# Earlier FFN jobs, a two-engine final projection and a re-searched prologue in a fused attention and FFN kernel

## The chip, the cores and the metric

The kernel runs on one core of a Trainium2 chip. Times are device microseconds (us) of one execution. A kernel's time is the median of its runs. The span of a profile runs from the first to the last instruction and is 1.7 to 1.9 us shorter than the time of the same run. Engines are written as in the profile: PE is TensorE's matmul pipe, PEld its weight loads, DVE is VectorE, ACT is ScalarE, POOL is GpSimd, SP issues DMAs (SPq is its queue).

## The reference

```python
x = A_x                                    # [1, 2048, 640] bf16
xn = layernorm(x)                          # over the last axis
# A: 32 query heads of 20, one shared key and value head (multi-query attention)
q = (xn @ wq) split in 32 heads;  k = xn @ wk;  v = xn @ wv
o = softmax(q k^T / sqrt(20)) v            # 32 x 2048 x 2048 scores
# B: FFN of width 1728
h = silu(xn @ w1)
return x + o @ wo + h @ w2
```

## The kernel before

The kernel is a generator. A scheduler in Python holds a cost model for each engine, decides for every engine a fixed order of instructions, and emits these orders with semaphores. On the chip nothing is decided any more: where the head of DVE's order, a reciprocal, waited 4.35 us in the changed kernel and began at 62.64, the phase copy behind it began only at 62.78.

The work is cut into 688 score steps (the queries of up to three heads against one block of 128 keys). For each, PE makes scores (L749 in the profile), ACT takes the exponential (L767), DVE takes over one head in many steps by an integer trick (L781, with phase copies in L842), and PE sums exponentials times values (L830). Sixteen key blocks make one group. Its sums U are evacuated by DVE, transposed by a DMA and normalised on POOL and DVE. In what follows this transpose is called the sum transpose. It is one DMA on SP's queue:

```python
    def norm_dma(self, g, rows):
        ...
        op = sc.dma("sp", lambda q: q.dma_start_transpose(self.UT[:, up, :, 0:rows], self.U[0:rows, up, :]),
                    [("U", up)], [("UT", up)], rows * QW * 2, sem=self.s_UT[up], name="uTd")
        ...      # four POOL instructions form sums and denominators in W, then on DVE:
        sc.new("dve", 0.22, lambda v: v.reciprocal(rl, w[:, :, :, DH]), [("W", 0), ("W", 1)], [("rL", up)],
               prio=U_PRIO, name=f"rcp{g}")
```

The prologue loads x, takes the statistics of 16 tiles of 128 rows, gets reciprocal square roots by Newton steps in batches of four tiles, normalises, transposes each tile (on PE, or by a DMA for the tiles in `DT`), and makes keys, values and queries. Then SP issues the loads of w1, wo, x (for the residual) and, last, the 14 pieces of w2 (2.2 MB). Fourteen DVE fills write a constant into the query buffer. Filler matmuls (L673, L686) stand where PE has no other work.

The end of the kernel, before: the FFN part and four fifths of the last chunk's projection are added by DVE into `yx`. After the last normalising, the last slice of `o` is transposed on PE and copied by DVE; then eight last-slice matmuls follow, and DVE adds all eight to `yx`:

```python
        if c == QC - 1:
            for i in range(4):
                for e in range(2):
                    self.misc.append(self.out_job(c, i, e, ffn=False, ks=range(DC - 1), src="yx", dst="yx"))
            self.misc.append(self.oT_last_job(c))
            for i in range(4):
                for e in range(2):
                    self.misc.append(self.out_job(c, i, e, ffn=False, ks=range(DC - 1, DC), src="yx"))
```

The softmax here doesn't subtract the row's maximum and nothing guards it: scores larger than these inputs give would overflow.

## Time and profile before

| | first set | with the changed kernel |
|---|---|---|
| median | 744.6 us (3 runs) | 744.75 us (4 runs) |
| range | 743.72 to 744.91 | 743.72 to 745.08 |
| profiled run | 747.35 us, span 745.6 | |

### The profile page before, as it was taken

To read this page: it belongs to the slowest core of one execution; us is meant where nothing else is said; L and a number is where in the kernel's file an instruction comes from. 1 tells how busy PE (TensorE), PEld (TensorE's weight loads), DVE (VectorE), ACT (ScalarE), POOL (GpSimd) and SP (SyncE) were. 2 spreads that over 40 slices of the span, in tenths; PEclk is the share of its full clock that TensorE was granted. 3 is DMA by queue.
4 is the path that set the end of the run, shared out by engine and by line. 5 is a ranking of instruction groups with operands and counts; after the bars stand their busy time and mean duration, and the time that the engine had idled before them with its cause. 6 is when DMAs were issued, how large, how long until landed. Compare 5 with 4: busy or idle time off the path is not lost.

```text
span 745.6 us, 17784 instructions
## 1 busy us (share of the span) xinstructions
PE 721.1 (97%) x6781; PEld 230.5 (31%) x6781; DVE 713.9 (96%) x1397; ACT 707.9 (95%) x780; POOL 111.7 (15%) x280
## 2 busy tenths in 40 slices
PE   8889999999999999999999999999999999999996
PEld 4332222233332222223333232222333322233332
DVE  7978999999999999999999999999999999999997
ACT  8968999999999999999999999999999999999962
POOL 5421112011112111110120111111111121111100
PEclk9979999999999999999999999999999999999999
DMA  6660000101003110000011211000002110000021
GB/s 188 158 248 15 17 20 16 22 16 15 9 15 62 52 46 16 9 16 1 8 16 25 70 44 37 16 8 8 10 8 43 51 45 8 8 9 8 9 43 36
DMA packets 55961, 27.05 MB, mean 36 GB/s; under 512 B 43686, under 2 KB 55238, under 8 KB 55878
## 3 DMA queue, kind: packets, MB, share of 16 engines
q1 hardware_dynamic: 54566, 25.87, 13.7%
q8 instruction: 55, 0.90, 0.5%
q10 hardware_dynamic: 1312, 0.05, 0.1%
q14 instruction: 28, 0.23, 0.1%
HBM read 11.36 MB, written 2.62 MB: 19 GB/s over the span
## 4 chain that ended last, share of the span: by engine, by line
PE 51%; DVE 20%; ACT 19%; issue 5%; POOL 2%; DMA 2%; DVEq 0%; ACTq 0%; POOLq 0%; SPq 0%
ACT sbt L767 18%; PE psall L830 17%; PE psall L749 17%; DVE sbt L781 9%; PE psall L1057 6%; PE psall L1119 5%; DVE sbt L842 5%; PE psall L1023 2%; PE psall L1124 2%; PE psall L673 2%; DVE sbt L1070 1%; DMA sbt<-sbt 1%; ACT sbt L1065 1%; DVE sbt L945 1%; DVE sbt L1352 1%
## 5 line engine op out<-in xcount | busy, mean ns | idle before, releaser
L767 ACT ACTIVATE sbt<-psall 128x1024 bf16<-128x1024 f32 (+2 forms) x688 | 674.4, 1117 | 21.7 <-PE psall L749 18.1
L781 DVE TENSOR_SCALAR sbt<-psall 128x512 int16<-128x512 f32 x608 | 406.4, 684 | 16.5 <-PE psall L749 10.2
L749 PE MATMUL psall<-sbt 32*128 32x512 bf16 x2048 | 269.5, 385 | 12.0 <-ACT sbt L767 6.0
L830 PE MATMUL psall<-sbt 128*32 128x512 bf16 x3434 | 264.7, 387 | 0.0
L842 DVE TENSOR_SCALAR sbt<-sbt 128x1536 int16<-128x1536 int16 (+2 forms) x436 | 223.9, 533 | 1.5
L749 PEld LDWEIGHTS psall<-sbt 32*128 32x128 bf16 x2048 | 69.7, 91 | 252.8 <-issue 86.8
L830 PEld LDWEIGHTS psall<-sbt 128*32 128x32 bf16 x3434 | 67.2, 95 | 112.4 <-issue 75.1
L915 POOL CAST sbt<-sbt 128x168 f32<-128x168 bf16 x42 | 17.3, 411 | 522.0 <-DMA sbt<-sbt 522.0
L1119 PE MATMUL psall<-sbt 128*128 128x320 bf16 x448 | 86.8, 303 | 0.0
L1057 PE MATMUL psall<-sbt 128*128 128x512 bf16 (+1 forms) x280 | 83.6, 384 | 1.6 <-DVE sbt L1070 1.0
L1119 PEld LDWEIGHTS psall<-sbt 128*128 128x128 bf16 x448 | 34.0, 97 | 43.4 <-issue 34.8
L1070 DVE SCALAR_TENSOR_TENSOR sbt<-sbt,psall 128x512 bf16<-128x512 bf16 (+1 forms) x56 | 38.2, 682 | 1.6 <-ACT sbt L1065 0.8
L931 POOL TENSOR_TENSOR sbt<-sbt 128x240 bf16<-128x240 f32 (+2 forms) x44 | 27.9, 635 | 65.7 <-DVE sbt L922 51.1
L1065 ACT ACTIVATE sbt<-psall 128x512 bf16<-128x512 f32 (+1 forms) x56 | 37.6, 671 | 0.0
L1124 PE MATMUL psall<-sbt 128*128 128x320 bf16 x160 | 31.6, 303 | 1.0 <-DVE sbt L1102 0.7
L1057 PEld LDWEIGHTS psall<-sbt 128*128 128x128 bf16 (+1 forms) x280 | 19.6, 98 | 41.3 <-issue 23.3
L945 DVE CAST sbt<-psall 128x512 bf16<-128x512 f32 x43 | 29.4, 684 | 0.9 <-PE psall L830 0.9
L1023 PE MATMUL psall<-sbt 128*128 128x512 bf16 (+1 forms) x95 | 28.4, 385 | 0.0
L917 POOL TENSOR_TENSOR sbt<-sbt 128x44 f32<-128x44 f32 x84 | 26.9, 320 | 6.6
L673 PE MATMUL psall<-sbt 128*32 128x512 bf16 (+9 forms) x86 | 26.6, 389 | 0.0
L912 POOL TENSOR_TENSOR sbt<-sbt 128x84 f32<-128x84 bf16 x42 | 18.0, 429 | 0.0
L1124 PEld LDWEIGHTS psall<-sbt 128*128 128x128 bf16 x160 | 12.0, 97 | 16.6 <-issue 11.7
(85 smaller groups left out, 198.4 us busy)
## 6 DMA issues: line engine op xcount, KB each, us to landing
sbt<-in_A_x_dram SPq DMA_DIRECT2D x32, 160.0 KB, 3.5
out_dram<-sbt SPq DMA_DIRECT2D x16, 160.0 KB, 1.8
sbt<-in_B_w_dram SPq DMA_DIRECT2D x5, 432.0 KB, 5.3
sbt<-sbt SPq DMA_DIRECT2D x105, 20.0 KB
sbt<-in_B_w_dram SPq DMA_DIRECT2D x13, 160.0 KB, 3.7
sbt<-sbt SPq DMA_TRANSPOSE x67, 2.5
sbt<-in_A_wo_dram SPq DMA_DIRECT2D x5, 160.0 KB, 6.1
sbt<-in_A_wq_dram SPq DMA_DIRECT2D x5, 140.0 KB, 3.6
```

The costliest lines, as they stand in the source:

```text
L673: return pe.matmul(self.bk(UBANK, 0, n, 0, 32), self.zero[:, 0:32], self.zero[:, 0:n], start=False, stop=False, tile_position=(0, 0), skip ...
L749: ins = pe.matmul(self.bk(par3 + j), self.kT[r:r + SLOT, kk, kt * P:(kt + 1) * P], self.qT[r:r + SLOT, h // 4, (x // H) % 2, :], start=Tru ...
L767: return a.activation(self.E[:, b0 * QW:(b0 + na) * QW], self.ps[:, par3 * BANK:(par3 + na) * BANK], AF.Exp, scale=ACT_SCALE)
L781: return v.tensor_scalar(self.Z[:, zs, zp * QW:(zp + 1) * QW], self.bk(bb), 0.0, ZMAX, ALU.max, ALU.min)
L830: return pe.matmul(self.bk(UBANK, 0, QW, q * SLOT, (q + 1) * SLOT), self.v[:, w, kt, :], x, start=start, stop=stop, tile_position=(0, q * ...
L842: sc.new("dve", t_dve_4x(w), lambda v, k=k: v.tensor_scalar(self.Y[:, zs, k, 0:n * QW], Z, float(PH[k + 1][0]), None, ALU.add), zk, [("Y", ...
L1023: return pe.matmul(self.bk(b, 0, QW, 0, rows), self.wq[:, k, lo:hi], self.xnT[:, k, c * QW:(c + 1) * QW], start=(k == 0), stop=(k == DC - 1))
L1057: return pe.matmul(self.bk(b, 0, QW, 0, rows), self.w1[:, k, fk * P:fk * P + rows], self.xnT[:, k, c * QW:(c + 1) * QW], start=(k == 0), s ...
L1065: sc.new("act", t_act(QW), lambda a: a.activation(t, src, AF.Tanh, scale=0.5), [("B", b)], [("tb", tp)], prio=X_PRIO, name=f"th{c}_{fk}")
L1070: sc.new("dve", t_dve_ps(QW), lambda v: v.scalar_tensor_tensor(out=self.hT[0:rows, fk, :], in0=t, scalar=1.0, in1=src, op0=ALU.add, op1=AL ...
L1119: return pe.matmul(self.bk(b, 0, 320), self.hT[0:rows, fk, i * P:(i + 1) * P], self.w2[0:rows, fk, e0:e0 + 320], start=(m == 0), stop=(m = ...
L1124: return pe.matmul(self.bk(b, 0, 320), self.oT[:, k, i * P:(i + 1) * P], self.wo[:, k, e0:e0 + 320], start=(m == 0), stop=(m == tot - 1))
```

## The change

Three intents. In the prologue, take work off DVE, use POOL, and let a search choose which engine does which statistics, Newton chain and normalising, and in what order PE takes its first jobs. In the middle, put four FFN jobs ahead of the previous chunk's output projection. At the end, sum half of the last chunk's projection in score banks that have come free (seeded with the residual by an identity matmul, "held" jobs) and evacuate by ACT and DVE together.

The constants in the cut below: `DT` lists the tiles that a DMA transposes, `PRO` the order of PE's first jobs, `ACT_STATS` the tiles whose statistics ACT takes, `NW_ENG` the engine of each batch's Newton chain, and `NORM_ENG` the engine that normalises each tile from tile 4 on. `LASTPV` puts value products first in the last 16 steps, `DVE_LAST` keeps DVE's exponential out of the last step, `FILL_EARLY` allows more fillers up to step `FILL_STEPS`, and `NEARLY` is the number of row tiles of the last chunk that still go through `yx`. Not shown are a fourth output buffer, whose output DMA ACT issues, and a cap on the work that a prologue job counts for when fillers are chosen.

```diff
+H_FIRST = 4
+NEARLY = 2
+LASTPV = 16
+DVE_LAST = 1
+FILL_EARLY = 0.95
+FILL_STEPS = 64
-PV_HOLD = 11
+PV_HOLD = 9
-DT = (4, 5, 6, 7, 11, 12, 13, 14, 15)
-NORM_P = 0.05
+DT = (4, 5, 8, 9, 10, 11, 12, 13, 14, 15)
+NORM_P = 0.5
-PRO = "v0 t8 t9 k2 t10 k3 k4 k5 q1 v1 k6 k7 d0 v2 v3"
-ACT_STATS = (2, 4, 6, 8, 9, 12)
-NW_ENG = ("dve", "pool", "pool", "dve")
-NORM_ENG = ("dve", "act", "dve", "dve", "pool", "pool", "dve", "act", "dve", "pool", "act", "act")
+PRO = "t6 v0 k2 t7 k3 k4 q1 v1 v2 k5 k6 k7 v3 d0"
+ACT_STATS = (4, 6, 9, 12, 14)
+NW_ENG = ("dve", "pool", "dve", "pool")
+NORM_ENG = ("pool", "pool", "pool", "pool", "dve", "act", "act", "dve", "act", "dve", "dve", "act")
 ... in the choice of PE's next work
+        if self.s_next >= self.T - LASTPV and pv_n:
+            choice = "PV"
 ... in the fillers
-        if room < 0.08 or self.busy_share(now) > FILL_BELOW:
+        if room < 0.08 or self.busy_share(now) > (FILL_BELOW if self.s_next > FILL_STEPS else FILL_EARLY):
 ... in the queue of jobs of a chunk (fs: projection of the chunk before, hs: FFN, ys: second FFN matmul)
-        for n, x in enumerate(fs + hs + ys):
+        for n, x in enumerate(hs[:H_FIRST] + fs + hs[H_FIRST:] + ys):
 ... at the end of the kernel
+    def hold_job(self, c, i, e):
+        ... two identity matmuls of the residual, then four fifths of the projection, left open in the bank
+        return Job(f"G{i}_{e}", mms, [("xres", i, e), ("idb",), ("oT", i), ("oTv", c, i), ("wo",)], lambda b: None,
+                   gate=lambda: self.s_next >= self.T and (c, i, e) in self.y_done, hold=(i, e))
 ...
-            self.misc.append(self.oT_last_job(c))
+            self.urgent.append(self.oT_last_job(c))
+            ... last-slice jobs alternate: held bank (ACT evacuates) and yx (DVE evacuates)
 ... in the prologue, the fills of the query buffer
+        pool(0.95, lambda g: g.tensor_scalar(self.tb[:, 0, :], self.zero[:, 0:QW], self.offq[:, :], 1.0, ALU.add, ALU.mult),
+             [("zero",), ("offq",)], [("tb", 0)])
+        ... for par in range(2): one DMA on SP's queue copies tb into all its places, ahead of the w1 loads
-        for par in range(2):
-            for ht in range(2 if par == 0 else 0, HT):
-                np_("dve", 0.31, lambda v, par=par, ht=ht: v.tensor_scalar(
-                    self.qT[:, ht, par, :], self.zero[:, 0:QW], self.offq[:, :], None, ALU.add), ...)
```

## The prediction

> **What bounds the kernel now.** I read four views, in this order: the engine totals, the windows of twenty microseconds, ScalarE's (ACT's) timeline through the start, and the timeline of the end.
>
> ```profile
> PE 721.1 (97%) x6781; PEld 230.5 (31%) x6781; DVE 713.9 (96%) x1397; ACT 707.9 (95%) x780; POOL 111.7 (15%) x280
> ```
>
> Three engines are each busy over 95% of 745.6 us, so no single engine is "the" bound of the middle. The windows confirm it (columns: stretch, length, then busy us of PE, PEld, DVE, ACT, POOL, granted clock, DMA share, GB/s):
>
> ```profile
> 20.00:40.00 20.00, 16.34 (x127) 6.84 (x126) 16.82 (x51) 16.78 (x19) 7.43 (x15) 0.88 0.71 201
> 40.00:60.00 20.00, 17.38 (x147) 6.57 (x145) 13.89 (x31) 12.30 (x13) 4.74 (x6) 0.78 0.50 177
> ...
> 200.00:300.00 100.00, 98.52 (x960) 29.32 (x959) 97.77 (x185) 100.00 (x106) 12.85 (x31) 1.00 0.16 36
> ```
>
> From 200 to 300 us ACT has no idle time and DVE 2%. A schedule cannot win much there. What it can win lies before 60 us, where ACT is idle 7.7 of 20 us and the clock drops to 0.78, and after the last exponential. ACT's timeline through the start (start, duration, line, shape, count, idle before and releaser; L767 is the exponential):
>
> ```profile
> 22.80 1.45 ACT L767 ACTIVATE sbt<-psall 128x1536 bf16<-128x1536 f32 x1
> 24.13 0.54 ACT L1326 ACTIVATE sbt<-sbt 128x400 bf16<-128x400 bf16 x1
> 25.08 1.73 ACT L1372 ACTIVATE sbt<-sbt 128x640 bf16<-128x640 bf16 x2 [0.41 <-DVE sbt L1409]
> 27.77 8.23 ACT L767 ACTIVATE sbt<-psall 128x1536 bf16<-128x1536 f32 x7 [0.96 <-PE psall L749]
> 36.44 1.02 ACT L767 ACTIVATE sbt<-psall 128x1024 bf16<-128x1024 f32 x1 [0.44 <-PE psall L830]
> 37.65 1.02 ACT L767 ACTIVATE sbt<-psall 128x1024 bf16<-128x1024 f32 x1 [0.19 <-PE psall L830]
> 39.90 1.02 ACT L767 ACTIVATE sbt<-psall 128x1024 bf16<-128x1024 f32 x1 [1.22 <-PE psall L749]
> 43.27 6.95 ACT L767 ACTIVATE sbt<-psall 128x1024 bf16<-128x1024 f32 x7 [2.35 <-PE psall L749]
> 53.21 3.77 ACT L767 ACTIVATE sbt<-psall 128x1024 bf16<-128x1024 f32 x4 [2.99 <-PE psall L749]
> 59.35 6.95 ACT L767 ACTIVATE sbt<-psall 128x1536 bf16<-128x1536 f32 x7 [2.36 <-PE psall L830]
> ```
>
> The brackets add to 0.41+0.96+0.44+0.19+1.22+2.35+2.99+2.36 = 10.9 us of idle ACT. Counting L767 (four before 24 us, then 7+1+1+1+7+4) gives 25 of the 688 score steps done by 59.35 us. The other 663 take from 59.35 to the last exponential's end at 733.3, 1.0165 us each. At that rate 25 steps are 25.4 us, so the kernel behaves as if its steady part began at 33.9 us, though its first exponential starts at 15.72.
>
> The end, all engines in order of time:
>
> ```profile
> 732.71 0.60 ACT L767 ACTIVATE sbt<-psall 128x512 bf16<-128x512 f32 x1 [2.24 <-PE psall L749]
> ...
> 735.68 0.69 DVE L945 CAST sbt<-psall 128x512 bf16<-128x512 f32 x1 [0.70 <-PE psall L830]
> ...
> 737.02 0.39 DVE L986 TENSOR_TENSOR sbt<-psall,sbt 128x80 bf16<-128x80 f32 x2
> 737.33 1.55 DVE L1142 SCALAR_TENSOR_TENSOR sbt<-psall,sbt 128x320 f32<-128x320 f32 x3
> 738.05 0.35 PEld L1097 LDWEIGHTS psall<-sbt 128*128 128x128 bf16 x4
> 738.18 0.39 PE L1097 MATMUL psall<-sbt 128*128 128x128 bf16 x4
> 738.79 0.41 DVE L1102 COPY sbt<-psall 128x512 bf16<-128x512 bf16 x1
> ...
> 739.61 2.48 DVE L1148 SCALAR_TENSOR_TENSOR sbt<-psall,sbt 128x320 bf16<-128x320 f32 x6 [0.40 <-PE psall L1124]
> 740.53 3.16 SPq L1152 DMA_DIRECT2D out_dram<-sbt  x4
> 742.44 0.89 DVE L1148 SCALAR_TENSOR_TENSOR sbt<-psall,sbt 128x320 bf16<-128x320 f32 x2 [0.35 <-DMA out_dram<-sbt]
> ```
>
> Twelve microseconds pass between ACT's last exponential and the end. They are one chain: last value products, evacuation (L945), reciprocal and normalising (L986), transposes (L1097), their copy (L1102), eight final evacuations on DVE alone (L1148), the output DMA.
>
> [...] PE is busy only 1.20, 0.79 and 1.34 of 2 us in the windows from 22 to 28, and the granted clock is 0.50 from 36 to 40, where L749 takes 0.61 instead of 0.39 us. The same happens around 50 and 56. [...] The trace has the engines at a share of 1.00 to 1.07 and 380 to 400 GB/s from 36 to 48 us.
>
> **The change, part by part.**
>
> *Prologue.* (a) Fourteen DVE fills of 128x512 (0.26 us apart where back to back) become one Pool instruction and two DMAs. That takes 14 x 0.26 = 3.6 us off DVE between 6.8 and 30 us, where DVE is on the chain, and adds 14 x 128 x 1 KB = 1.83 MB of transfers. At the 385 GB/s of the trace these are 4.8 us, queued ahead of the w1 load. The saturated stretch then ends about 5 us later than its 49 us; the first FFN matmul is at 60.4 us, so I expect this to hide. (b) ACT's statistics go from six tiles to five, and tile 2, one of the first four that gate everything, moves to DVE. ACT's pair for one tile takes 1.7 us; DVE's statistics take 2 x 0.40 + 0.11 = 0.9. Without the three fills between them, I expect the first exponential at about 15.2, 0.5 earlier. (c) Normalising of tiles 4 to 7 goes to Pool behind its own Newton chain. The chain here is 3.4 us and each normalise 0.88. Before, Pool waited for the last statistics until 14.49, and steps 4 to 7 started only at 27.3 after transposes queued at SP. I expect them near 23. (d) The job order puts the value jobs v2 and v3 ahead of the last key and query jobs. The gaps of 2.99 and 2.36 us before 53 and 59 are exponentials stopped by full exponential buffers: PE runs fill matmuls, then a burst of value products (L830) as soon as the value evacuations (L1504) land at 50 and 57. Earlier value jobs attack just these 5.35 us. (e) More filler matmuls in the first 64 steps, up to 0.95 busy, [...] they attack 1.22+2.35+0.44+0.19 = 4.2 us. Of the 10.9 us of gaps I give half back, 5.0 us with the earlier start included, because work of 3.6 us leaves DVE but the tile transposes and their issue (9 before, 10 after, about 1.3 us each) stay serial.
>
> *Middle.* Four FFN jobs lead each chunk, so the head of the job queue is not blocked by the previous chunk's output projection. Filler (L673) in the windows shows where PE had nothing: 3.99 us from 220 to 240, nearly nothing at 400 to 420 (0.60) and none at 560 to 600. So only one of the three boundaries has a hole. Four FFN jobs are 20 matmuls at 0.216 = 4.3 us, which just fills it. ACT was fully busy there, so the gain is only the job backlog that ends earlier: after 702 us PE is on the chain nearly alone and ACT is idle 2.55 us before 720. I give it 1.5 us.
>
> *End.* (f) No DVE exponential in the last step, and value products ahead of jobs in the last sixteen: four L1124 matmuls (0.65 us on the chain at 733.80) and one DVE round (0.68 plus part of L842's 1.08) leave, one 512-column ACT exponential is added (1.08 instead of 0.60). Net about 0.9 us. (g) The transposes become urgent and three L1142 leave DVE: from the normalising's end at 737.41 to the copy's start at 738.79 were 1.38 us; transposes 0.39 and two handovers of about 0.2 make 0.8. Gain 0.6. (h) The final eight evacuations: from the first matmul at 739.26 to the last end at 743.33 are 4.07 us, with 0.35 waiting for a buffer that an output DMA still reads. With four on DVE (0.41 each) and four on ACT (0.42, by the line through its 512 and 1024 columns, 0.60 and 1.08) and a fourth output buffer, 0.35 + 4 x 0.42 = 2.0. Gain 2.0. The eight identity matmuls (8 x 0.15 = 1.2 us of PE) lie beside the evacuation chain from 735.7 to 738. Sum 3.5, less 0.2 for a held job that delays the transposes: 3.3.
>
> Total: 5.0 + 1.5 + 3.3 = 9.8, so 744.6 - 9.8 = 734.8; I round up to 735.5, since a searched order fits its own model better than the chip.
>
> **The rivals.** *The prologue gain doesn't arrive.* For it: Pool now has two Newton chains and four normalises in series (2 x 3.4 + 3.5 = 10.3 us), the DMA engines carry 1.83 MB more while tile transposes may still land[...]. Against it: Pool is 15% busy. Then only 4 to 5 us remain: 740. *All gaps close.* With all 10.9 us of ACT gaps, 1.7 us of statistics off ACT and the end as above, the time is about 730; 2% is 14.9 us, so 729.7 is just beyond even that. *The held banks hurt.* If the reordering piles jobs behind the last score step, PE is the bound to the end and the identity matmuls are on the chain: the end gains 1.5 rather than 3.3, total 737. *PE-bound middle.* If extra fillers or the shifted FFN jobs take PE time from real work, the middle gives nothing: 737.
>
> **Range and chances.** The middle of these is 735.5; eight times in ten between 730.5 and 740.5. Over 2% faster needs everything at once: 0.07. Within 2%: 0.91. Slower by over 2% would need a new stall of 15 us: 0.02.
>
> **What would show it.** Right: steps 4 to 7 near 23 us; 30 or more exponentials done by 59.35; granted clock above 0.9 from 40 to 60; no filler near 220 to 240; the last exponential's end about 6.5 us earlier (near 726.8); at most 9.5 us from there to the end, with four evacuations of 128x320 on ACT and no wait for an output buffer. Wrong: the gaps of L767 before 60 us still add to 8 us or more; a half clock remains; FFN jobs wait for w1; the wait after the last value product grows.

The sum came to 5.0 + 1.5 + 3.3 = 9.8 us, so 744.6 - 9.8 = 734.8, rounded up to 735.5. The reason of term (e) is cut too, as no run shows it; its 4.2 us are part of the 10.9 us of gaps, of which half is given back. "The engines" with a share of 1.00 to 1.07 are the DMA engines.

## More of the kernel before

A plain load is taken to land after all traffic issued before it (`dma_t`). A transpose is taken to land 1.6 us after its issue, whatever the DMA engines carry:

```python
        if op.dma:
            if op.name in ("oTd", "xTd", "uTd"):
                self.dma_t = op.end
            self.dma_t = max(getattr(self, "dma_t", 0.0), op.end) + op.mode / 230e3
            op.avail = op.end + 1.6 if op.name in ("oTd", "xTd", "uTd") else max(op.end + 2.0, self.dma_t + 1.6)
```

Besides the lines in the prediction, the argument needs SP's queue (start, duration of the issuing, line, operation, count), which I had read only for its first half:

```profile
18.66 12.73 SPq L1430 DMA_TRANSPOSE sbt<-sbt  x9
31.43 2.61 SPq L1435 DMA_DIRECT2D sbt<-in_B_w_dram  x5
...
39.41 7.40 SPq L1268 DMA_DIRECT2D sbt<-in_B_w_dram  x14
46.85 5.34 SPq L1039 DMA_DIRECT2D sbt<-sbt  x7
60.87 1.22 SPq L904 DMA_TRANSPOSE sbt<-sbt  x1
```

Here the w2 loads (L1268) have been issued by 46.8 us, and the first sum transpose (L904) leaves at 60.9 us, long after. There is no traffic left when it goes: the DMA share is 0.00 in every 2 us from 54 to 62.

## The result, and the profile after

Ratios here and below are the mean time of one kernel's fast runs over that of the other's of the same rounds, with a 95% interval; so they are not quite the ratio of the medians that I quote.

| | before | after |
|---|---|---|
| median | 744.75 us (4 runs) | 745.8 us (4 runs) |
| range | 743.72 to 745.08 | 744.75 to 746.59 |
| ratio | | 1.0016 [0.9997, 1.0034] |

The predicted time was 735.5, the range 730.5 to 740.5. The time did not move. The gain was not absent, though; it was made and given back. ACT's timeline of the changed kernel through the start (L782 is now the exponential, L764 the scores):

```profile
29.26 1.45 ACT L782 ACTIVATE sbt<-psall 128x1536 bf16<-128x1536 f32 x1 [2.52 <-PE psall L764]
...
45.13 16.54 ACT L782 ACTIVATE sbt<-psall 128x1024 bf16<-128x1024 f32 x17 [1.94 <-PE psall L764]
65.03 1.02 ACT L782 ACTIVATE sbt<-psall 128x1024 bf16<-128x1024 f32 x1 [3.35 <-PE psall L764]
...
67.45 1.94 ACT L782 ACTIVATE sbt<-psall 128x1024 bf16<-128x1024 f32 x2 [0.91 <-PE psall L764]
70.25 2.05 ACT L782 ACTIVATE sbt<-psall 128x1024 bf16<-128x1024 f32 x2 [0.87 <-PE psall L764]
```

Seventeen exponentials run without a break from 45 to 61.7 us, where the kernel before had breaks of 2.99 and 2.36 us. The break just before, 2.35 us in the kernel before, is 1.94 here. Then comes a new break of 3.35 us and two of 0.9, together 5.1 us. I count the exponentials done by a given time, since one exponential later is worth 1.0165 us (the prediction's rate). "Before" has two profiles, the first of a run of 747.35 us and the second (the run before_again below) of 745.79 us:

| exponentials done by | 60 us | 65 | 70 | 80 | 200 | 700 |
|---|---|---|---|---|---|---|
| before, first profile | 26 | 31 | 35 | 45 | 162 | 658 |
| before_again | 28 | 32 | 37 | 47 | 164 | 659 |
| after | 30 | 31 | 34 | 44 | 162 | 658 |

At 60 us the changed kernel leads by 2 to 4 exponentials. At 80 us it is behind by 1 to 3. So whatever happens from 61.7 to 71 us takes back all that the prologue had won. SP's queue, DVE, POOL and PE at that place follow. First SP:

```profile
19.40 17.30 SPq L1476 DMA_TRANSPOSE sbt<-sbt  x10
36.75 1.43 SPq L1487 DMA_DIRECT2D sbt<-sbt  x2
38.21 5.54 SPq L1490 DMA_DIRECT2D sbt<-in_B_w_dram  x5
...
48.60 7.43 SPq L1314 DMA_DIRECT2D sbt<-in_B_w_dram  x14
56.07 1.28 SPq L919 DMA_TRANSPOSE sbt<-sbt  x1
```

The tile transposes end at 36.70 instead of 31.39, the two fills (L1487) take 1.43 us to issue, and so w2 (L1314) is issued 9 us later than before. The first sum transpose (L919) stands behind it. What it transposes had been evacuated by DVE in an instruction (L960) that began at 51.75 and took 0.68, so the data was ready at 52.4; it was issued at 56.07 and, with the DMA engines still full (share 1.26 from 56 to 60), the trace puts its landing 5.1 us after its issue (the median of all 42 such transposes is 2.4). The evacuation:

```profile
51.75 0.68 DVE L960 CAST sbt<-psall 128x512 bf16<-128x512 f32 x1
```

Then POOL:

```profile
61.27 0.33 POOL L930 CAST sbt<-sbt 128x168 f32<-128x168 bf16 x1 [16.73 <-DMA sbt<-sbt]
```

and DVE, whose order puts the reciprocal (L937) ahead of the phase copies (L857) that PE needs:

```profile
57.60 0.68 DVE L796 TENSOR_SCALAR sbt<-psall 128x512 int16<-128x512 f32 x1
62.64 0.23 DVE L937 RECIPROCAL sbt<-sbt 128x12 f32<-128x12 f32 x1 [4.35 <-POOL sbt L932]
62.78 0.50 DVE L857 TENSOR_SCALAR sbt<-sbt 128x1536 int16<-128x1536 int16 x1
```

and PE, whose value products (L845) wait for a phase copy:

```profile
63.33 1.04 PE L845 MATMUL psall<-sbt 128*32 128x512 bf16 x8 [2.92 <-DVE sbt L857]
```

This is one chain, read upwards from ACT: ACT waits for scores, PE for a phase copy, DVE for POOL's sums, POOL for a DMA. The windows (columns as in the prediction) show what it costs besides:

```profile
52.00:56.00 4.00, 3.94 (x36) 1.06 (x35) 3.96 (x8) 4.00 (x6) 0.00 (x0) 1.00 1.07 386
56.00:60.00 4.00, 3.84 (x31) 1.12 (x29) 2.28 (x5) 4.00 (x5) 0.00 (x0) 1.00 1.26 338
60.00:62.00 2.00, 0.41 (x4) 0.10 (x3) 0.00 (x0) 1.68 (x2) 0.65 (x3) 1.00 0.22 50
62.00:64.00 2.00, 0.67 (x8) 0.14 (x8) 1.36 (x4) 0.00 (x0) 1.58 (x4) 0.60 0.08 21
64.00:66.00 2.00, 2.00 (x13) 0.37 (x13) 2.00 (x3) 0.97 (x2) 1.83 (x3) 0.50 0.02 4
66.00:68.00 2.00, 1.86 (x14) 0.21 (x6) 1.97 (x5) 1.09 (x3) 1.83 (x3) 0.50 0.03 8
```

PE is busy 1.08 of 4 us from 60 to 64, with one idle stretch of 2.92 us, and the granted clock is 0.60 from 62 to 64 and 0.50 from there to 68. The DMA share is over 1.00 until 60 us; in the kernel before it was at 1.00 or more from 34 to 48 only, and 0.05 from 52 to 56.

The end of the changed kernel:

```profile
734.53 0.69 DVE L960 CAST sbt<-psall 128x512 bf16<-128x512 f32 x1 [1.33 <-PE psall L845]
...
737.10 0.42 DVE L1117 COPY sbt<-psall 128x512 bf16<-128x512 bf16 x1 [0.57 <-PE psall L1112]
737.59 0.45 PE L1197 MATMUL psall<-sbt 128*128 128x320 bf16 x2 [0.52 <-DVE sbt L1117]
...
738.41 1.33 PE L1139 MATMUL psall<-sbt 128*128 128x320 bf16 x8
738.75 1.62 ACT L1166 ACTIVATE sbt<-psall 128x320 bf16<-128x320 f32 x4 [6.46 <-PE psall L1139]
738.88 1.68 DVE L1169 SCALAR_TENSOR_TENSOR sbt<-psall,sbt 128x320 bf16<-128x320 f32 x4 [1.36 <-PE psall L1139]
```

The evacuation is shared as intended: four on ACT, four on DVE, no wait for a buffer. From the first last-slice matmul (738.41) to the last evacuation's end (738.88 + 1.68 = 740.56) are 2.15 us, against 4.07. But the fourth held job (L1197) begins only behind the copy (L1117), and the eight last matmuls stand behind it.

### The profile page after: what moved, and what is told of

Its sections match the earlier page's. It is cut to its first block, busy times and chain, and to the rows that moved or that the text cites. A ratio compares the mean times of both kernels' runs of the same rounds, so it can differ in the third digit from the quotient of the medians.

```text
span 743.2 us, 17728 instructions
## 1 busy us (share of the span) xinstructions
PE 708.9 (95%) x6725; PEld 229.5 (31%) x6783; DVE 703.5 (95%) x1369; ACT 708.3 (95%) x780; POOL 111.3 (15%) x282
## 4 chain that ended last, share of the span: by engine, by line
PE 62%; ACT 23%; DVE 8%; issue 5%; DMA 1%; POOL 1%; ACTq 0%; DVEq 0%; POOLq 0%
ACT sbt L782 20%; PE psall L764 20%; PE psall L845 19%; PE psall L1134 8%; PE psall L1072 6%; DVE sbt L796 3%; ACT sbt L1080 2%; PE psall L1139 2%; PE psall L1038 2%; PE psall L701 2%; DVE sbt L857 2%; PE psall L688 1%; DMA sbt<-sbt 1%; PE psall L1519 1%; DVE sbt L960 0%
## 5 line engine op out<-in xcount | busy, mean ns | idle before, releaser
L782 ACT ACTIVATE sbt<-psall 128x1024 bf16<-128x1024 f32 (+2 forms) x688 | 675.7, 1124 | 18.6 <-PE psall L764 17.9
L764 PE MATMUL psall<-sbt 32*128 32x512 bf16 x2048 | 269.6, 385 | 12.6 <-ACT sbt L782 8.3
L845 PE MATMUL psall<-sbt 128*32 128x512 bf16 x3427 | 260.4, 386 | 4.3 <-DVE sbt L857 2.9
L857 DVE TENSOR_SCALAR sbt<-sbt 128x1536 int16<-128x1536 int16 (+2 forms) x434 | 221.7, 530 | 1.3
L764 PEld LDWEIGHTS psall<-sbt 32*128 32x128 bf16 x2048 | 69.2, 91 | 252.4 <-ACT sbt L782 108.9
L845 PEld LDWEIGHTS psall<-sbt 128*32 128x32 bf16 x3427 | 66.0, 94 | 112.8 <-issue 73.6
L1134 PE MATMUL psall<-sbt 128*128 128x320 bf16 x448 | 87.1, 303 | 0.3 <-DVE sbt L1151 0.3
L1072 PE MATMUL psall<-sbt 128*128 128x512 bf16 (+1 forms) x241 | 75.3, 386 | 5.2 <-issue 3.0
L1134 PEld LDWEIGHTS psall<-sbt 128*128 128x128 bf16 x448 | 33.7, 97 | 44.3 <-issue 35.3
L960 DVE CAST sbt<-psall 128x512 bf16<-128x512 f32 x43 | 29.2, 680 | 2.3 <-PE psall L845 2.3
L1139 PE MATMUL psall<-sbt 128*128 128x320 bf16 x144 | 29.2, 303 | 0.0
L1038 PE MATMUL psall<-sbt 128*128 128x512 bf16 (+1 forms) x78 | 24.4, 383 | 2.6 <-issue 1.3
L688 PE MATMUL psall<-sbt 128*32 128x512 bf16 (+7 forms) x80 | 23.5, 353 | 0.0
L701 PE MATMUL psall<-sbt 128*128 128x512 bf16 (+2 forms) x67 | 17.6, 409 | 4.7 <-DVE sbt L1552 3.2
```

What stands on the lines that cost most here:

```text
L701: return pe.matmul(self.bk(b, 0, n), self.zero[:, 0:P], self.zero[:, 0:n], start=True, stop=True)
L764: ins = pe.matmul(self.bk(par3 + j), self.kT[r:r + SLOT, kk, kt * P:(kt + 1) * P], self.qT[r:r + SLOT, h // 4, (x // H) % 2, :], start=Tru ...
L782: return a.activation(self.E[:, b0 * QW:(b0 + na) * QW], self.ps[:, par3 * BANK:(par3 + na) * BANK], AF.Exp, scale=ACT_SCALE)
L845: return pe.matmul(self.bk(UBANK, 0, QW, q * SLOT, (q + 1) * SLOT), self.v[:, w, kt, :], x, start=start, stop=stop, tile_position=(0, q * ...
L857: sc.new("dve", t_dve_4x(w), lambda v, k=k: v.tensor_scalar(self.Y[:, zs, k, 0:n * QW], Z, float(PH[k + 1][0]), None, ALU.add), zk, [("Y", ...
L1038: return pe.matmul(self.bk(b, 0, QW, 0, rows), self.wq[:, k, lo:hi], self.xnT[:, k, c * QW:(c + 1) * QW], start=(k == 0), stop=(k == DC - 1))
```

## The experiments

The main theory: the prologue's gain is real, and it is lost at 62 to 71 us because the first sum transpose is now caught in the weight loads. Its rivals: (1) the prologue gained nothing, and the lead at 60 us is chance or an artefact of which run was profiled; (2) the loss comes from POOL, which by then scales wo (five L1534 from 63.70) and disturbs DVE; (3) it is only SP's fixed order, not the traffic; (4) late w2 loads are good by themselves, whatever the transposes do; (5) the fills or the fillers cost what they saved. Twelve runs were made, ten of edited kernels and one more of each of the two kernels themselves, all with correct results. Each comparison is by the ratio to the kernel before on the same chip. A comparison across batches goes by these ratios.

**The kernel before, once more (before_again).** No edit.

> The kernel before, unchanged, for a second profile: the one I read was 745.6 us in span while the median run is about 743. If the two profiles differ by 2 us, the difference should sit in one place (a half clock stretch before 65 us), with the same 26 exponentials done by 60 us within one. If it sits in the middle instead, differences of 2 us between two profiles mean nothing.

Time 745.79 us (one run). Its gaps of ACT from 24 us to 60 us are 0.40+1.17+0.64+0.67+0.48+0.16+1.82+1.44+0.87 = 7.65 us, against 10.9 in the first profile. The difference is of this kind:

```profile
44.11 6.96 ACT L767 ACTIVATE sbt<-psall 128x1024 bf16<-128x1024 f32 x7 [1.82 <-PE psall L749]
52.51 3.78 ACT L767 ACTIVATE sbt<-psall 128x1024 bf16<-128x1024 f32 x4 [1.44 <-PE psall L749]
57.15 6.96 ACT L767 ACTIVATE sbt<-psall 128x1536 bf16<-128x1536 f32 x7 [0.87 <-PE psall L830]
```

The same three gaps were 2.35, 2.99 and 2.36 us in the first profile. That profile had a clock of 0.50 from 36 to 40, from 50 to 52 and from 56 to 58. This one lost its clock earlier (0.50 from 28 to 32) and has 1.00 from 34 to 60. So some 3 us of the idle time that I had set out to win back were in one run and not in the next. The clock differs there too; no run isolates it as the cause. The count of 28 exponentials by 60 us is also outside the 26, within one, that I had expected. Rival 1 has a part of the truth: the lead at 60 us may be 2 exponentials and not 4.

**The w2 loads behind the first sum transpose (a_w2after).** Only SP's order differs; the other engines' orders are the same. The first w2 load also waits until the transpose has landed.

```diff
         self.sc.run()
+        sp = self.sc.order["sp"]
+        w2 = [o for o in sp if o.sem is self.s_w["2"]]
+        rest = [o for o in sp if o.sem is not self.s_w["2"]]
+        i = [o.name for o in rest].index("uTd")
+        w2[0].deps = set(w2[0].deps) | {rest[i]}
+        while rest[i + 1].name == "qdma":
+            i += 1
+        self.sc.order["sp"] = rest[:i + 1] + w2 + rest[i + 1:]
```

> The changed kernel with one edit: on SP's queue the fourteen loads of w2 stand behind the first transpose of value sums and the seven query copies; every other engine has the same instructions in the same order. Theory A (the prologue gain of 4 exponentials is given back because the first transpose of value sums is issued 3.6 us late behind the w2 loads and lands in 5.1 instead of 2.4 us): the 3.35 us gap of ACT at 61.7 to 65.0 closes, 34 exponentials done by 65 us instead of 31, and the time falls by 3 to 5 us against the changed kernel, to about 741. Rival B (the stall at 62 us has another cause, Pool's or DVE's order, or the later steps are bound elsewhere so that nothing is carried through): gap stays or time stays within 1 us of the changed kernel.

Time 741.22 us, ratio 0.9941 [0.9926, 0.9957]. The changed kernel had 1.0016, so this one order is worth 0.75%, some 5.6 us. The two ratios come from different batches and each has an interval of over 0.3%. The medians differ by 4.6 us and the two profiled runs by 3.8, so 4 to 6 us is as much as can be said. ACT at the same place (L790 is the exponential):

```profile
44.53 17.47 ACT L790 ACTIVATE sbt<-psall 128x1024 bf16<-128x1024 f32 x18 [1.99 <-PE psall L772]
...
63.18 2.09 ACT L790 ACTIVATE sbt<-psall 128x1024 bf16<-128x1024 f32 x2 [0.69 <-PE psall L772]
65.83 4.80 ACT L790 ACTIVATE sbt<-psall 128x1024 bf16<-128x1024 f32 x5 [0.55 <-PE psall L772]
```

SP and POOL:

```profile
51.78 1.45 SPq L927 DMA_TRANSPOSE sbt<-sbt  x1
57.54 0.33 POOL L938 CAST sbt<-sbt 128x168 f32<-128x168 bf16 x1 [13.65 <-DMA sbt<-sbt]
```

The break of 3.35 us is 0.69, and the clock stays at 1.00 from 40 to 70. Note that the transpose is no faster here: it lands 5.7 us after its issue, with a DMA share of 1.03 from 48 to 52 us and of 1.35 from 52 to 56 (the fills and the loads of w1, wo and x had been issued before). What it gains is that it is issued 4.3 us earlier and has no w2 load in front of it. There are 34 exponentials by 65 us (after: 31) and 661 by 700 (658): the lead, once kept, is carried to the end. Rival 2 falls here as the cause of the gap: POOL's scaling of wo still runs beside DVE, now from 59.97, and DVE's two phase copies beside it are as slow as before (2.04 us for two; 2.03 in the changed kernel), and no such gap follows.

**The transpose between the w2 loads (a_utmid).** To tell queue order from traffic, the transpose alone moves, in front of the ninth of 14 loads.

```diff
+        u = next(o for o in sp if o.name == "uTd")
+        sp.remove(u)
+        i = [j for j, o in enumerate(sp) if o.sem is self.s_w["2"]][8]
+        sp.insert(i, u)
```

> The changed kernel with the first transpose of value sums moved up on SP's queue between the eighth and ninth w2 load, so that it is issued near 53 us, with the w2 traffic still in flight. If the wait in SP's issue order is the larger part (3.6 of 6.3 us), the gap at 62 us shrinks from 3.35 to under 1 us and the transpose still takes 4 us or more to land. If the traffic is the larger part, the gap stays at 2 us or more.

Time 745.34 us (742.64 to 747.08, a wide spread), ratio 1.0000 [0.9981, 1.0019]. The transpose was issued at 53.81, 2.3 us earlier than in the changed kernel, yet it landed 6.4 us later, at 60.2, and ACT's gap was still 2.51 + 0.74 us:

```profile
53.81 1.56 SPq L924 DMA_TRANSPOSE sbt<-sbt  x1
63.91 1.02 ACT L787 ACTIVATE sbt<-psall 128x1024 bf16<-128x1024 f32 x1 [2.51 <-PE psall L769]
```

This profile is of the fastest of the four runs (742.64), so the typical gap may be longer. Being issued 2.3 us earlier thus brought the landing forward by 1.0 us only: of the 2.3 us that it gained by leaving SP before the last six loads, 1.3 were lost again between issue and landing. Rival 3 falls as the only cause. Two things stay open. No run separates the loads in front of the transpose from those behind it, and none issues the transpose from another queue, so whether it is held up by its place in SP's queue or by the other traffic on its way is not shown.

**The same move in the kernel before (b_w2after), a control.** The edit of a_w2after.

> Control: the kernel before with the same move of the w2 loads behind the first transpose of value sums. There the loads' issue ends at 47 us and the transpose is issued at 59, long after. Theory A says nothing is gained: within 1 us of the kernel before. If it gains 3 us or more, late w2 loads help by themselves and theory A falls.

Time 745.8 us, ratio 1.0011 [0.9996, 1.0025]. Nothing is gained where no transpose stood in the loads' way. Rival 4 falls.

**Only the new end (endonly).** All prologue constants as before, DVE fills, FFN order as before.

```diff
-H_FIRST = 4
+H_FIRST = 0
+... PV_HOLD, DT, NORM_P, PRO, ACT_STATS, NW_ENG, NORM_ENG, fills and fillers as in the kernel before
```

> The kernel before with only the new end (held banks, two engines for the last evacuation, value products first in the last 16 steps): the prologue's settings, the DVE fills and the FFN order as before. Theory: the end gains 1.5 to 3 us by itself, so 742 to 743 and at most 10.9 us from the last exponential's end to the end of the kernel, against 12.3 before. Rival: the reordering lets jobs pile up, the last exponential ends later, and the time is that of the kernel before within 1 us.

Time 744.28 us, ratio 0.9976 [0.9959, 0.9994], so about 1.8 us. The three last held jobs are carried out after the copy, and the last matmuls wait for them:

```profile
733.61 0.44 PE L1197 MATMUL psall<-sbt 128*128 128x320 bf16 x2 [0.52 <-DVE sbt L1117]
...
736.07 1.33 PE L1139 MATMUL psall<-sbt 128*128 128x320 bf16 x8
```

That is the rival "the held banks hurt" of the prediction, in part: 2.5 us between copy and last matmuls.

**The held jobs' false dependence (a_tailfix, on a_w2after).** A held job reads four of the five slices of oT, but lists a tag that the copy of the fifth slice writes. So each held job that comes later in PE's order than the transposes waits for a copy it does not read.

```diff
-        return Job(f"G{i}_{e}", mms, [("xres", i, e), ("idb",), ("oT", i), ("oTv", c, i), ("wo",)], lambda b: None,
+        return Job(f"G{i}_{e}", mms, [("xres", i, e), ("idb",), ("oTv", c, i), ("wo",)], lambda b: None,
```

> The changed kernel with w2 behind the first transpose, and the held-bank jobs no longer named as readers of the slice that the last copy writes (they read the other four slices). The fourth held job then runs while the copy runs. Expected: from the copy's end to the first last-slice matmul 0.3 us instead of 0.85, end of the kernel 0.5 to 0.8 us earlier counted from the last evacuation of value sums (8.65 us there): 7.9 to 8.1. Rival: PE is the bound there and nothing moves.

Time 739.21 us (739.04 to 741.43), ratio 0.9927 [0.9913, 0.9940]: the fastest, 5.9 us under the 745.13 of the kernel before in its batch. The held job now lies ahead of the copy (L1125), and the copy's end at 732.30 is followed at 732.49 by the last matmuls (L1147):

```profile
731.67 0.43 PE L1205 MATMUL psall<-sbt 128*128 128x320 bf16 x2
731.88 0.42 DVE L1125 COPY sbt<-psall 128x512 bf16<-128x512 bf16 x1 [0.57 <-PE psall L1120]
...
732.49 1.33 PE L1147 MATMUL psall<-sbt 128*128 128x320 bf16 x8
```

From the last U evacuation's start to the end are 8.0 us (729.30 to 737.3), against 8.65 in a_w2after and 9.85 in before_again.

**FFN jobs not first (a_w2noH, on a_w2after).**

```diff
-H_FIRST = 4
+H_FIRST = 0
```

> The changed kernel with w2 behind the first transpose of value sums, and the previous chunk's output projection first in each chunk again, as before. My prediction gave the FFN-first order 1.5 us, by filling the hole of PE near 220 to 230 us. If that holds, this kernel is 1 to 2 us slower than the one with FFN first (741.2), shows about 4 us of filler matmuls between 220 and 240 and fewer exponentials from 300 us on. Rival: the hole cost nothing because ACT and DVE were busy in it; same time within 0.7 us, same count of exponentials at 300 to 700 us within 1.

Time 743.5 us, ratio 0.9975 [0.9963, 0.9988] against 0.9941 [0.9926, 0.9957], in another batch: by the ratios the FFN order is worth some 2.5 us, with wide margins. The way that I had named is not it. The filler from 220 to 240 us, 3.99 us before, is 0.34 here without the FFN order and 0.00 with it; so the hole was already closed by something else. And of the two exponentials by which this profile lies behind that of a_w2after at 300 us (264 against 266), one is missing at 80 us already (47 against 48), where the edit cannot act yet: in the first chunk there is no earlier projection to go ahead of. So the profiles bear out 1 us at most, the times 2.5, and the mechanism is open.

**Fills back on DVE (a_qzdve, on the changed kernel).**

```diff
-        pool(0.95, lambda g: g.tensor_scalar(self.tb[:, 0, :], ...), ...)
-        ... the two fill DMAs
+        ... the fourteen DVE fills of the kernel before
```

> The changed kernel with the fourteen fills of query offsets back on DVE and without the two DMAs of 1.83 MB; w2 in its old place. Theory A: the queue of loads ends about 1.4 us earlier in issue and 5 us earlier in traffic, so the first transpose lands earlier and the gap of 3.35 us at 62 us shrinks by 1.5 to 3 us; DVE has 3.6 us more work before 45 us. Time 743 to 745. If the gap stays at 3 us, the DMAs of the fills were not its cause.

Time 748.08 us, ratio 1.0043 [1.0028, 1.0059], 2 us slower than the changed kernel. There is no gap near 62 us any more, but new ones came at 42 and 48:

```profile
42.07 2.00 ACT L782 ACTIVATE sbt<-psall 128x1024 bf16<-128x1024 f32 x2 [2.35 <-PE psall L764]
48.36 1.94 ACT L782 ACTIVATE sbt<-psall 128x1024 bf16<-128x1024 f32 x2 [4.29 <-PE psall L764]
```

So giving back the fills' 1.83 MB of traffic does not make this kernel faster. Whether moving the fills off DVE helps by itself is not shown: with other instructions the scheduler made another order on all engines, so the run is not a clean test.

**Newton steps out of POOL's way (dveorder, on a_tailfix).** This tests why steps 4 to 7 came at 29.26 and not near 23. In the changed kernel DVE's second Newton chain (nine instructions, L1437 to L1455) takes 4.3 us, from 18.90 to 23.2:

```profile
18.90 0.50 DVE L1437 TENSOR_SCALAR sbt<-sbt 128x4 f32<-128x4 f32 x1
19.43 0.83 DVE L1438 TENSOR_SCALAR sbt<-sbt 128x4 int32<-128x4 int32 x1
20.30 0.81 DVE L1444 TENSOR_TENSOR sbt<-sbt 128x4 f32<-128x4 f32 x1
21.14 0.82 DVE L1446 SCALAR_TENSOR_TENSOR sbt<-sbt 128x4 f32<-128x4 f32 x1
...
22.45 0.16 DVE L1444 TENSOR_TENSOR sbt<-sbt 128x4 f32<-128x4 f32 x1
```

The same operation (L1444) takes 0.81 at 20.30 and 0.16 at 22.45. POOL ran four normalises in a row from 18.50 to 21.96, some 0.87 each; the last three of them thus end near 20.23, 21.10 and 21.96, and the three long DVE rows end at 20.26, 21.11 and 21.96. The statistics (L1398) took 0.48 beside POOL at 18.50 and 0.44 at 23.24 without it. So some of DVE's instructions are slow beside POOL's normalises in this trace; why is not shown. The experiment moves the nine instructions.

```diff
+        dv = self.sc.order["dve"]
+        nw = [o for o in dv if o.name == "nw"][9:]
+        mv = nw + [o for o in dv if o.name in ("norm8", "norm11")]
+        dv = [o for o in dv if o not in mv]
+        i = max(j for j, o in enumerate(dv) if o.name == "vev0")
+        self.sc.order["dve"] = dv[:i + 1] + mv + dv[i + 1:]
+        ... on ACT the fourth exponential ahead of two normalises
```

> The version with w2 late and the held jobs freed (739.2), with one reordering: on DVE the Newton steps of tiles 8 to 11 and the two normalises behind them stand after the first value evacuation, and on ACT the fourth exponential stands ahead of two normalises. No instruction is added or taken away. Theory: the Newton steps took 4.3 us in the changed kernel, against 1.6 to 1.9 for the same nine instructions elsewhere, because Pool's four normalises (18.5 to 22.0 us) ran at the same time[...]; moved behind them they take 1.9 us or less, PE is no longer idle for 3.2 us at 22.5, and the fifth exponential (29.2 to 29.7 us in the earlier profiles of this prologue) starts 1.5 to 2.5 us earlier. Rival: the steps are slow by themselves with the PE clock or DMA traffic, and take 4 us again. The time: 0 to 2 us below 739.2, as tiles 8 to 11 come 1 us later.

The nine took 1.8 us (25.11 to 26.93) instead of 4.3, now that POOL's four normalises (19.80 to 23.24) were over; the rival, that they are slow by themselves, falls. The time was 741.52 us, ratio 0.9949 [0.9936, 0.9961], which is not better than a_tailfix's 0.9927. The fifth exponential came at 29.02, 11.0 us after the first instead of 12.3, but tiles 8 to 11 were now later, and the clock was lost twice (0.50 at 32 to 34 and at 48 to 50). My expectation of 0 to 2 us below a_tailfix was missed. A likely reading, which no run isolates, is that what was won for one batch of tiles was lost on the next.

**Fewer fillers, first try (fe78, on a_tailfix).**

```diff
-FILL_EARLY = 0.95
+FILL_EARLY = 0.78
```

> The version with w2 late and the held jobs freed, with the filler threshold of the first 64 steps back at 0.78 from 0.95. My prediction counted on more fillers[...]. If that holds, this shows fewer fillers before 80 us, a stretch at half clock between 40 and 60 us, and 1 to 2 us more. Rival: the half clock in the first profile of the kernel before was luck of the moment (its second profile had full clock from 36 to 60 us with the same fillers); then same time within 1 us.

Time 749.42 us, ratio 1.0045 [1.0028, 1.0062]. This run failed as a test of fillers, and repeats the main finding by accident. In the scheduler's new order eight query copies follow the first sum transpose, not seven. The rule of a_w2after put w2 behind all of them, the eighth was ready only at 72.71, and so w2 was issued at 73.82, in front of the second sum transpose:

```profile
73.82 7.07 SPq L1322 DMA_DIRECT2D sbt<-in_B_w_dram  x14
80.94 1.27 SPq L927 DMA_TRANSPOSE sbt<-sbt  x1
```

```profile
86.25 0.23 DVE L945 RECIPROCAL sbt<-sbt 128x12 f32<-128x12 f32 x1 [8.32 <-POOL sbt L940]
```

DVE stood for 8.3 us before that reciprocal, and ACT had a gap of 7.48 us. The same mechanism, at another transpose, from the order of one queue.

**Fewer fillers, mended (fe78b).** The same, with w2 behind exactly seven query copies.

```diff
-        while rest[i + 1].name == "qdma":
-            i += 1
+        i += 7
```

> The threshold test again without its flaw: in the run before, the w2 loads had landed behind an eighth query copy that waited until 74 us, and so in front of the second transpose of value sums, whose wait stopped ACT for 7.5 us. Here they stand behind exactly seven query copies. Expected: no gap at 80 us, 45 or more exponentials by 80 us, 741 to 743. If more fillers are worth 1 to 2 us, it stays 1 to 3 us above the version with 0.95 (0.9927 of before); if not, within 1 us of it.

Time 740.12 us (737.41 to 745.10), ratio 0.9938 [0.9905, 0.9971] against 0.9927. The intervals overlap, and the four runs spread over 7.7 us. The clock from 28 to 32 us is 0.63 with fewer fillers and 0.94 with more, but from 36 to 40 it is 1.00 and 0.66. Whether the denser fillers are worth anything is not settled; it is small.

**The changed kernel, once more (after2).** No edit.

> The changed kernel once more, unchanged, on the chip of this call: a second trace and an interval from five rounds. Expected: within 0.3% of the kernel before, the first transpose of value sums issued near 56 us and landing after 61, and an ACT gap of 3 us or more at 61 to 65 us. If the gap is not there in a second trace while the time is the same, theory A loses its ground.

Time 745.64 us, ratio 1.0012 [0.9998, 1.0025]. The stall repeats: the sum transpose was issued at 57.03, POOL began at 61.98, ACT's gaps were 2.71, 0.71 and 0.34 (I had expected 3 us or more for the first), and 31 exponentials were done by 65 us.

The kernels that carry the argument, side by side:

| kernel | median us | ratio to before | exponentials by 65 us | by 700 us |
|---|---|---|---|---|
| after / after2 | 745.8 / 745.64 | 1.0016 / 1.0012 | 31 / 31 | 658 / 658 |
| a_w2after | 741.22 | 0.9941 | 34 | 661 |
| a_tailfix | 739.21 | 0.9927 | 35 | 663 |

## Why the prediction was right or wrong

It was wrong: 735.5 predicted, 745.8 measured, and outside the range. "Within 2%" with a chance of 0.91 was right.

**The step that failed** is in part (a): "The saturated stretch then ends about 5 us later than its 49 us; the first FFN matmul is at 60.4 us, so I expect this to hide." I asked only when the loaded weights are first needed. I did not ask what else has to pass through the same queue while they are on their way. The first sum transpose had to: its data was ready at 52.4 us in the changed kernel, while in the kernel before it was issued only at 60.87. And the stretch ended at about 60 us, not 54, since the tile transposes ended 5.3 us later too. Taking the w2 loads alone out of the transpose's way (a_w2after) gives 4 to 6 us. The prediction's first rival named the right traffic, but the wrong victims ("while tile transposes may still land").

**The second error is in the base.** I took gaps from a profile of a 747.35-us run and subtracted their closing from a median of 744.6. "Of the 10.9 us of gaps I give half back": in before_again, whose 745.79 us lie at the median of its batch (745.95), they were 7.65. As only half was given back, this overstated the gain by about half of the difference, 1.6 us. A third slip touches the range: the rival "all gaps close" adds up to 744.6 - 10.9 - 1.7 - 3.3 = 728.7, not "about 730", so it would have been over 2% faster.

**The reading of the clock** was also looser than it looks. It sets the low PE shares from 22 to 28 us beside the clock of 0.50 from 36 to 40. In the first profile the clock is 1.00 from 20 to 34 us, so the low PE shares from 22 to 28 are not followed by the drop at 36. The longest idle time that PE's timeline lists between 20 and 36 us is 1.21 us. What made the clock drop there (0.77 from 34 to 36, 0.50 from 36 to 40) is not shown.

Point by point:

- (b) First exponential near 15.2: no. It came at 16.71, and in before_again at 16.59, against 15.72 in the first profile. Its start hangs on the run: the same 44 filler matmuls ahead of the first score step took 11.16 us in the profile of after and 12.69 in that of a_w2after, and the first exponential began at 16.71 and 18.26.
- (c) Steps 4 to 7 near 23: wrong, 29.26. I priced POOL's chain, and not that DVE's Newton chain is slower beside POOL's normalises (4.3 us, against 1.8 in dveorder; one instruction 0.81 us instead of 0.16). PE then stands for 3.23 us behind DVE. But dveorder, which took the two apart, brought the step forward by 1.3 us only, of 6.3 us missing; the rest is open.
- (d) and (e), the gaps near 43, 53 and 59: right for the last two, which are gone; the first is 1.94 us instead of 2.35. The exponentials run through from 45.13 to 61.67, 30 are done by 60 us, and the clock is 1.00 from 40 to 60, though it is 0.50 from 26 to 28 and from 36 to 38. The prediction had asked for "30 or more exponentials done by 59.35" and a clock above 0.9.
- Middle, 1.5 us: a_w2noH gives at most 1 us by the profiles and 2.5 by the times. Right as a size, not as a mechanism: the hole from 220 to 240 was closed without it.
- End, 3.3 us: the tail from the last exponential's end was 10.9 us (732.28 to 743.2) against 12.2 (before_again, 731.78 to 744.0), a gain of 1.3. Term (h) was 1.9 us, as predicted (2.0). Term (g) was 0.8 (0.56 us from normalising's end to the copy, against 1.38), as predicted (0.6). Term (f) failed: last exponential to U evacuation took 2.25 us against 2.37, so 0.1 and not 0.9. "Less 0.2 for a held job" was 0.8, by the false dependence. The final DMA part was 0.35 longer (2.64 against 2.27) and the two normalises 0.2.

Do these sizes account for the 10.3 us that were missing (745.8 less 735.5)? The stall is 4 to 6, the held job's dependence about 1.0 (a_tailfix against a_w2after, 0.0014 of 745), and term (f) with the DMA part 1.15. That is 6 to 8. The remaining 2 to 4 us are the base (about 1.6 by the prediction's own halving) and the parts (b) and (c) that did not come; no run separates them. The terms come from different batches, so this is a check of size and not a proof.

## What to carry to other kernels

When a transfer is added or delayed and looks hidden, ask not only when its own data is needed but what other small transfer, in the same queue or only at the same time (these runs do not tell which of the two counts), now has to go through it, and follow that one to the engines behind it. In this kernel, with its fixed orders on every engine, one late small DMA stopped the whole chain (ACT idle for 3.35 us in the changed kernel, for 7.48 in fe78), and making the front of a kernel faster can bring the collision about: the first sum transpose's data was ready at 52.4 us here, and its transpose left only at 60.87 before. Before you subtract what a profile shows from a median, look whether the profiled run was a median one.
